# A statically scheduled kernel: the scheduler model holds the shared VectorE/GpSimd port longer, and its plan is searched anew with more weight on low TensorE activity

## Chip, cores, metric

One core of one Trainium2 chip. The metric is the device time of one execution in microseconds, as the median of several. Ratios are the mean time of one kernel's fast runs over that of the other's of the same rounds, so not quite the ratio of the medians quoted beside them.

## The reference

Four residual blocks on x of shape 1×2048×512: attention A, linear attention B, then both again.

```python
def _A_ref(x, wq, wk, wv, wo):            # 32 heads of 16, one shared K and V
    q = ...; k = x @ wk; v = x @ wv
    p = _softmax(einsum("bhqd,bkd->bhqk", q, k) * Dh ** -0.5)
    return (p @ v) @ wo                   # reshapes cut
def _B_ref(x, wqkv, wo):
    phi = lambda t: where(t > 0, t + 1, exp(t)) + 1e-6
    ...                                   # num = phi(q) @ (phi(k)^T v), den = phi(q) . sum phi(k)
    return (num / den) @ wo
x = x + A(layernorm(x)); x = x + B(layernorm(x))      # twice
```

The weight lies in A: 32 heads × 2048 × 2048 scores to exponentiate, twice. "Layer" below is one A with its B. The "boundary" is the stretch from the last exponential of layer 1 to the twenty-first of layer 2, the "tail" what follows the last exponential of layer 2.

## The kernel before

A Python list scheduler runs before launch. It plays the whole program on a clock of its own, with a duration for each op, and so decides the order on each engine and, for the attention tiles, which engine exponentiates what. The orders are then emitted with semaphores. The chip cannot change them. The scores of both layers are 4096 tiles of 512 columns. ScalarE takes sets of three or two (`exp`), VectorE takes single tiles (`P1`, an integer approximation), then adds three shifted copies of four such tiles, two by a wide op of its own (`xo`) and the last by four small GpSimd ops (`xp`); TensorE weighs all four.

```python
PLAN = (                      # every 6 us of the scheduler's clock: priorities, look-aheads, limits
    (0.0, {'LX': 0.338, 'HOLD': 0.836, 'LEAD': 16, ...}),
    (6.0, {'MF': 0.758, 'PX': 0.523, ...}),
    ...                       # cut: 245 entries
)
# Sched._try: may engine e start op o now? (cut)
if e == DV and o.port and self.tfree[PO] > self.now + 1e-9 or e == PO and self.dport > self.now + 1e-9:
    continue                  # VectorE's port ops and GpSimd exclude each other
...
# run(): engines are asked in this order at each event
self.engs = [PE, AC, DV, PO, SP]
...
# ScalarE's exponential, VectorE's P1, its shift, GpSimd's pieces (cut)
oe = add(AC, tac(m * 512), lambda e: e.activation(PTA[...], bank(...), ACTF.Exp, scale=SCALE), ...)
o = add(DV, tdv(512), lambda e: e.tensor_scalar(out=PTD[...512], in0=bank(db), ...), name="P1", ...)
o = add(DV, tdv(512 * m, 0.26), ..., name="xo", port=True)        # 2048 columns, SBUF to SBUF
add(PO, PXO[0] + 512 * PXO[1], ..., name="xp", pair=PXM)
...
# layer B, each of 16 token tiles: numerator's phi(q) times 1/den, on whichever engine is free
o = add((DV, PO) if PQE else DV, {DV: tdv(512), PO: PHS}, ..., name="pqn", port=True)
```

`tdv(512)` and the wide shift are 0.600 us in the model, `tac(1536)` 1.331 and `tac(1024)` 0.905, PHS 1.27.

The softmax here doesn't subtract the row's maximum and nothing guards it: scores larger than these inputs give would overflow.

## Time and profile before

| | before |
|---|---|
| median of 3 runs | 1495.28 us (1494.65 to 1497.23) |
| profiled run, first to last instruction | 1497.1 us |
| TensorE, ScalarE, VectorE, GpSimd busy | 97, 97, 92, 57% |

In profile lines PE is TensorE, PEld its weight loads, ACT ScalarE, DVE VectorE and POOL GpSimd; `out<-in` names the tiles, L1035 is line 1035 of the kernel. `ps_all` holds TensorE's results (in PSUM), which the program cuts into banks of 512 columns; `PTA` and `PTD` hold the exponentials (in SBUF). The prediction shows the page's busy line, its clock, its chain and the windows around the half clock. The table of waits (who waited for whom: total us, times, longest) says that TensorE's score loads wait mostly for a bank that an exponential still reads, then for P1:

```profile
PEld ps_all L1035 <- ACT PTA L1192: 220.1, 589, 0.9
...
PEld ps_all L1035 <- DVE PTD L1252: 88.5, 284, 0.7
```

And the view of line 1578, the multiplication `pqn` (count: shortest/median/longest ns, first and last start):

```profile
L1578 POOL TENSOR_TENSOR pqT<-pqT,e_buf x20: 1157/1162/1172, 733.1 to 1491.0; 128x512 bf16<-128x512 bf16 x20
L1578 DVE TENSOR_TENSOR pqT<-pqT,e_buf x12: 684/692/1048, 734.1 to 1492.3; 128x512 bf16<-128x512 bf16 x12
```

The two engines share the 32 multiplications; GpSimd needs 1.7 times as long for one. VectorE's longest, 1048 ns, began 0.5 us before a GpSimd op ended.

### The profile page before, as it was taken

Reading aid. Unit: us, or ns where it says so; the run is one execution under the profiler, and the core shown is the slowest. Engines: PE = TensorE matmul, PEld = TensorE weight load, DVE = VectorE, ACT = ScalarE, POOL = GpSimd, SP = SyncE. Lnnn points to the kernel's source line nnn. Section 1 sums busy time; section 2 is a strip of 40 time slices with the busy share of each in tenths; the row PEclk is TensorE's granted clock in tenths of the full one; section 3 lists DMA queues with packets and bytes.
Section 4 is the critical chain, followed back from the end, with each engine's and each line's share of the span. In section 5 each row is a group of like instructions: output and inputs, shape, how many; then the busy total and the mean of one; then the engine's idle time right before and its main releaser. Section 6 shows DMA issues by size and latency. Waiting matters only on the chain.

```text
span 1497.1 us, 38261 instructions
## 1 busy us (share of the span) xinstructions
PE 1459.2 (97%) x16245; PEld 492.0 (33%) x16255; DVE 1376.5 (92%) x2433; ACT 1444.9 (97%) x1426; POOL 853.2 (57%) x1360
## 2 busy tenths in 40 slices
PE   7999999999999999999899999999999999999998
PEld 4322333322333333333442333333333232333334
DVE  7999998999988999899798999989999899989987
ACT  7999999999999999999698999999999999999996
POOL 3556656565563655565544556566565456565654
PEclk9999999999999999999998999999999999999999
DMA  3000000000000000000000000000000000000001
GB/s 118 26 9 5 9 12 5 5 5 4 14 6 7 5 5 17 9 8 9 2 1 5 5 9 8 9 5 5 5 5 15 6 5 5 9 16 8 6 9 57
DMA packets 46251, 17.71 MB, mean 12 GB/s; under 512 B 39936, under 2 KB 45568, under 8 KB 46080
## 3 DMA queue, kind: packets, MB, share of 16 engines
q1 hardware_dynamic: 46080, 15.27, 4.3%
q8 instruction: 127, 2.08, 0.6%
q14 instruction: 44, 0.36, 0.1%
HBM read 5.28 MB, written 2.10 MB: 5 GB/s over the span
## 4 chain that ended last, share of the span: by engine, by line
PE 58%; ACT 23%; DVE 19%; issue 1%; POOL 0%; DMA 0%; SPq 0%; ACTq 0%
PE ps_all L1072 24%; PE ps_all L1035 23%; ACT PTA L1192 20%; DVE PTD L1252 10%; PE ps_all L768 7%; DVE PTD L1323 5%; PE ps_all L772 2%; PE ps_all L1093 2%; DVE Eo L1084 1%; DVE stats L840 1%; ACT e_buf L1576 1%; ACT e_buf L1439 1%; ACT e_buf L1577 1%; DVE e_buf L1446 0%; DVE x_sb L1431 0%
## 5 line engine op out<-in xcount | busy, mean ns | idle before, releaser
L1192 ACT ACTIVATE PTA<-ps_all 128x1536 bf16<-128x1536 f32 (+1 forms) x1178 | 1357.8, 1292 | 18.7 <-PE ps_all L1035 15.0
L1313 POOL TENSOR_SCALAR PTD<-PTD 128x512 uint16<-128x512 uint16 x1124 | 683.2, 618 | 489.2 <-DVE PTD L1323 317.6
L1252 DVE TENSOR_SCALAR PTD<-ps_all 128x512 uint16<-128x512 f32 x1142 | 751.1, 680 | 69.9 <-PE ps_all L1035 65.4
L1035 PE MATMUL ps_all<-QT,Kr 32*128 32x512 bf16 x4141 | 658.6, 385 | 9.9 <-ACT PTA L1192 3.6
L1072 PE MATMUL ps_all<-PTD,Vaug 128*32 128x512 bf16 x4568 | 616.2, 386 | 5.8 <-DVE Eo L1084 5.2
L1072 PE MATMUL ps_all<-PTA,Vaug 128*32 128x512 bf16 x2954 | 533.8, 387 | 0.2
L1323 DVE TENSOR_SCALAR PTD<-PTD 128x2048 uint16<-128x2048 uint16 x577 | 403.6, 711 | 2.2
L1035 PEld LDWEIGHTS ps_all<-QT,Kr 32*128 32x128 bf16 x4141 | 169.1, 91 | 493.0 <-ACT PTA L1192 220.1
L1072 PEld LDWEIGHTS ps_all<-PTD,Vaug 128*32 128x32 bf16 x4568 | 158.6, 94 | 218.1 <-issue 141.5
L1072 PEld LDWEIGHTS ps_all<-PTA,Vaug 128*32 128x32 bf16 x2954 | 131.8, 94 | 145.8 <-issue 114.2
L768 PE MATMUL ps_all<-wqkv_sb,xnT 128*32 128x512 bf16 x960 | 72.5, 382 | 0.1
L1448 POOL TENSOR_SCALAR e_buf<-e_buf 128x512 f32<-128x512 f32 x60 | 36.8, 613 | 43.1 <-ACT e_buf L1439 23.9
L1446 DVE TENSOR_SCALAR e_buf<-ps_all 128x512 f32<-128x512 f32 x60 | 40.9, 685 | 14.3 <-ACT e_buf L1439 14.2
L1439 ACT ACTIVATE e_buf<-ps_all 128x512 f32<-128x512 f32 x64 | 41.7, 655 | 9.7 <-PE ps_all L772 6.5
L1450 POOL TENSOR_TENSOR pqT<-e_buf 128x512 bf16<-128x512 f32 x30 | 38.0, 1268 | 11.8 <-DVE PTD L1323 8.0
L1450 POOL TENSOR_TENSOR pk_tok<-e_buf 128x512 bf16<-128x512 f32 x30 | 38.1, 1272 | 10.5 <-DVE PTD L1323 9.4
L1084 DVE COPY Eo<-ps_all 128x512 f32<-128x512 f32 x62 | 42.3, 682 | 1.5 <-PE ps_all L1072 1.3
L840 DVE BATCH_NORM_STATS2 stats<-x_sb 128x6 f32<-128x512 bf16 x64 | 42.9, 678 | 0.5 <-DMA x_sb<-in_A_x_dram 0.2
L1093 PE MATMUL ps_all<-identf,Eo 128*128 128x128 f32 x256 | 42.4, 289 | 0.0
L768 PE MATMUL ps_all<-wo_sb,OT 128*32 128x512 bf16 x480 | 37.7, 382 | 0.0
L1578 POOL TENSOR_TENSOR pqT<-pqT,e_buf 128x512 bf16<-128x512 bf16 x20 | 23.2, 1164 | 25.1 <-ACT e_buf L1577 6.5
L929 POOL TENSOR_SCALAR Vaug<-Vaug 128x32 bf16<-128x32 bf16 x48 | 14.9, 311 | 32.1 <-DVE Vaug L925 15.5
(102 smaller groups left out, 686.2 us busy)
## 6 DMA issues: line engine op xcount, KB each, us to landing
out_dram<-x_sb SPq DMA_DIRECT2D x16, 128.0 KB, 1.7
OT<-Osb SPq DMA_TRANSPOSE x120, 2.4
xnT<-xn_buf SPq DMA_TRANSPOSE x120, 2.3
wqkv_sb<-in_B_wqkv_dram SPq DMA_DIRECT2D x4, 384.0 KB, 3.1
x_sb<-in_A_x_dram SPq DMA_DIRECT2D x3, 256.0 KB, 3.4
x_sb<-in_A_x_dram SPq DMA_DIRECT2D x1, 768.0 KB, 7.9
wq_sb<-in_A_wq_dram SPq DMA_DIRECT2D x1, 512.0 KB, 6.4
x_sb<-in_A_x_dram SPq DMA_DIRECT2D x1, 512.0 KB, 8.7
```

Source lines behind the costliest of these rows:

```text
L768: i = e.matmul(out[32 * c:32 * c + 32], lhsT=lhsT[:, 32 * c:32 * c + 32], rhs=rhs, start=start, stop=stop, skip_group_check=True)
L840: add(DV, tdv(512), lambda e: e.bn_stats(stats[:, t, 0:6], x_sb[:, t, :]), reads=[("x", t)], writes=[("st", t)], prio=prio, name="bn")
L1035: x = e.matmul(bank(b0 + k), lhsT=Kr[r, m, kt * P:(kt + 1) * P], rhs=QT[r, self.units[u][0] % 2, gs, q0:q0 + n], start=True, stop=True)
L1072: return e.matmul(ps[32 * c:32 * c + 32, 7 * 512:8 * 512], lhsT=Vaug[:, kt, r, :], rhs=src() if callable(src) else src, start=opened[0], s ...
L1084: return (e.copy if oe.eng == AC else e.tensor_copy)(Eo[:, he.idx, :], bank(7))
L1093: i = e.transpose(bank(ht.idx, P, qs * P), Eo[:, he.idx, qs * P:(qs + 1) * P], identf[:])
L1192: oe = add(AC, tac(m * 512), lambda e: e.activation(PTA[:, hp.idx, 0:m * 512], bank(SETS[s][0], m * 512), ACTF.Exp, scale=SCALE), deps=[o] ...
L1252: o = add(DV, tdv(512), lambda e: e.tensor_scalar(out=PTD[:, hp.idx, i * 512:(i + 1) * 512], in0=bank(db), scalar1=SCALE * LOG2E * 128.0, ...
L1313: return e.tensor_scalar(out=PTD[:, ht.idx, i * 512:(i + 1) * 512], in0=PTD[:, hp.idx, i * 512:(i + 1) * 512], scalar1=float(SHIFT[r]), sc ...
L1323: return e.tensor_scalar(out=PTD[:, ht.idx, 0:512 * m], in0=PTD[:, hp.idx, 0:512 * m], scalar1=float(SHIFT[r]), op0=ALU.add, **kw)
L1439: o1 = add(AC, tac(512), lambda e: e.activation(e_buf[:, he.idx, :], bank(h.idx), ACTF.Exp), deps=[o], uses=[h], acq=[he] if fast else [he ...
L1450: add(PO, PHS, lambda e: e.tensor_tensor(out=dst, in0=sh(e_buf[:, hr.idx, :]), in1=sh(e_buf[:, he.idx, :]), op=ALU.add), deps=[o2, o3], us ...
```

## The change

Intent: make the model's port rule as slow as the chip's, and search the plan anew with an objective that punishes stretches in which TensorE does little (the prediction shows one of 13.65 us at half clock). The code (parameters cut; most of the 245 entries differ):

```diff
+PBL = 0.04
+R0 = 0
 PLAN = (
-    (0.0, {..., 'NT0': 3, 'DMIN': 1, ..., 'MF': 0.285, ..., 'PX': 2.788, ...}),
+    (0.0, {..., 'NT0': 5, 'DMIN': 2, ..., 'MF': 0.413, ..., 'PX': 0.523, ...}),
     ... (cut)
-            if e == DV and o.port and self.tfree[PO] > self.now + 1e-9 or ...
+            if e == DV and o.port and self.tfree[PO] > 0.0 and self.tfree[PO] + PBL > self.now + 1e-9 or ...
+        if e == PO:
+            self.at(end + PBL, None)
-   ... self.add_pv(p, ..., dep[0 if r and not split else i], r, 1)
+   ... self.add_pv(p, ..., c["p1"][-1] if R0 and not r else dep[0 if r and not split else i], r, 1)
```

The new wait of 0.04 us (PBL) before a VectorE port op is called the hold below. R0 is 0, so the last edit does nothing. Two lines were added near the top and two in the body: old line 1252 is new 1256, 1323 is 1327, 1578 is 1582.

## The prediction

> **What bounds the kernel now.** I read the page's busy shares first, then the slices, the groups by line, the table of waits, and short windows of the timeline.
>
> ```profile
> PE 1459.2 (97%) x16245; PEld 492.0 (33%) x16255; DVE 1376.5 (92%) x2433; ACT 1444.9 (97%) x1426; POOL 853.2 (57%) x1360
> ...
> PEclk9999999999999999999998999999999999999999
> ...
> PE 58%; ACT 23%; DVE 19%; issue 1%; POOL 0%; DMA 0%; SPq 0%; ACTq 0%
> ```
>
> Three engines are nearly full, and the chain of waits passes between them. There is no single bound. A Python list scheduler lays out, before launch, one fixed order for each engine. ScalarE (ACT) takes the exponentials of score tiles in sets of three or two; VectorE (DVE) takes the others through an integer approximation: one op from PSUM ("P1", line 1252), two shifts over four tiles (line 1323), while GpSimd (POOL) does the fourth shift in pieces (line 1313). What matters is how far the chip departs from the times the scheduler assumed, since the orders cannot adapt. For that I compare starts of neighbours, which are not hidden by the overlap of ends. An exponential of three tiles follows its neighbour after 1331 ns at the median, one of two after 904 ns, and a P1 takes 600 ns from end to end: just the assumed durations. One group is off:
>
> ```profile
> L1252 DVE TENSOR_SCALAR PTD<-ps_all 128x512 uint16<-128x512 f32 x1142 | 751.1, 680 | 69.9 <-PE ps_all L1035 65.4
> L1323 DVE TENSOR_SCALAR PTD<-PTD 128x2048 uint16<-128x2048 uint16 x574 | 402.6, 713 | 2.2
> ```
>
> Both are assumed at 600 ns, yet the shift's mean is 713 ns and P1's 680. Sorting the 574 shifts by whether a GpSimd op still ran at their start gives two piles: 286 that start 150 to 200 ns before a GpSimd op ends have a mean of 728 ns; the 195 whose start meets no GpSimd op have 679. From end to end a shift takes 600 or 647 ns, mean 632. One pair in the timeline (VectorE, then GpSimd):
>
> ```profile
> 805.61 0.72 DVE L1323 TENSOR_SCALAR PTD<-PTD 128x2048 uint16<-128x2048 uint16 x1
> 806.26 1.27 DVE L1252 TENSOR_SCALAR PTD<-ps_all 128x512 uint16<-128x512 f32 x2
> ```
> ```profile
> 803.98 1.81 POOL L1313 TENSOR_SCALAR PTD<-PTD 128x512 uint16<-128x512 uint16 x3 [0.63 <-DVE PTD L1323]
> ```
>
> GpSimd ends at 803.98+1.81 = 805.79, 0.18 us after the shift's start; the shift ends at 806.33, and the next op starts 0.65 us after it instead of 0.60. Last, the dip in PEclk:
>
> ```profile
> 780.00:810.00 30.00, 30.00 (x313) 9.20 (x310) 26.93 (x46) 28.62 (x26) 15.73 (x26) 1.00 0.01 1
> 810.00:830.00 20.00, 19.52 (x147) 4.54 (x144) 14.83 (x25) 14.21 (x13) 8.34 (x15) 0.66 0.05 9
> 830.00:860.00 30.00, 29.64 (x311) 9.27 (x310) 29.51 (x53) 29.79 (x27) 17.89 (x30) 1.00 0.03 5
> ```
>
> The clock record has one stretch of 13.65 us at half speed, from 813.0. ScalarE (fourth busy number) is idle for 20-14.21 = 5.8 us there; around it it is idle for 60-58.41 = 1.6 us in 60, or 0.5 in 20. So the stretch cost about 5.3 us.
>
> **What the Trainium skill says.** "SBUF — State Buffer", section "Who interferes with whom": VectorE's second pair of SBUF ports is GpSimd's pair; it is an exclusive lock held for a whole instruction, and the later of the two blocks. `tensor_scalar` in a two-port mode takes it, an op with at most one SBUF input outside those modes does not. The trace agrees: shifts behind a GpSimd op lose 49 ns, P1 (PSUM input) shows 683 ns with GpSimd running and 678 without. "VectorE: DVE Perf Modes", section "Mode 4×_2P — both tricks at once", explains why the shift is such an op: 16-bit SBUF to SBUF, one source; it moves 2048 elements in the 600 ns that P1 takes for 512. "TensorE: Matmul & The Clock Gate", section "What's actually happening": a free-running window of activity of about 3.4 us halves the clock when TensorE was little used and restores it after a busy one. The trace agrees that the clock has only 1.0 and 0.5, and that one thin spell was enough.
>
> **The change part by part.** The emitted instructions are the same in kind; only the scheduler's clock and 200-odd lines of tuned parameters differ. The new R0 is 0 and does nothing. So I compare the two built programs' counts and orders.
>
> (a) The port. The model now forbids a VectorE port op until 0.04 us after GpSimd's end: close to the 47 ns measured. The hardware wait is not abolished: 574 × (632-600) = 18.4 us on VectorE stay, unless another op (a P1) runs in the gap. What improves is that the plan expects it, so TensorE's in-order queue is no longer stuck behind a late P1 while ScalarE's next scores wait. I bound the prize: in 20-700 and 840-1450 us the starts after ScalarE's exponentials are later than 1331/904 ns by 18.8 + 15.6 = 34.4 us in sum. Some of this is planned (evictions, projections). I choose a quarter as recovered: -9 us.
>
> (b) Shares. The exponentials go from 598 of three and 580 of two to 601, 582 and one of a single tile: 14 of 4096 tiles move from VectorE to ScalarE (P1 1142 to 1128). ScalarE gains 3×1.331 + 2×0.904 + 0.48 = +6.3 us; its other ops nearly cancel. VectorE sheds 14×0.60 = 8.4 us of P1, some six shifts, and (d). As ScalarE is as full as TensorE, I count two thirds as showing in the end: +4 us.
>
> (c) Clock. If no stretch of half speed remains, -5.3 us. A search that punishes thin spells makes this likely, not certain, as the window is free-running and the new order's spells are unknown; at 0.55, -3 us. The small filler matmuls rise from 44 to 100 (11 to 25 groups), full ones fall from 28 to 17: the new plan still has thin places and pads more.
>
> (d) A side effect: when GpSimd becomes free, it may start at once but VectorE not for 0.04 us, so GpSimd takes all 32 multiplications of line 1578 (before 20, VectorE 12). They cost 1162 against 692 ns; in the last layer 16 of them at 1.12 us apart are 17.9 us, about as long as that phase (first normaliser 1474.5, last VectorE one 1492.3). I count +1 us.
>
> (e) TensorE: four small matmuls share one pass of about 0.217 us. The approximate tiles shed 56 matmuls (-3.0 us), the exponentials add 14 (+0.8), fillers 56 small (+3.0) and 11 full (-2.4), scores 23 (+1.7 at three a pass): 0.
>
> Sum: 1495.3 - 9 + 4 - 3 + 1 = 1488.3 us.
>
> **Rivals.** *The wait is only moved.* VectorE still loses 47 ns behind GpSimd and now the model also leaves gaps, so VectorE takes fewer tiles and ScalarE more. For it: 14 tiles moved, and VectorE is idle for 8% anyway, so a 47 ns loss may have been absorbed already. Against it: waits of the score loads on P1 already sum to 88.5 us in 284 cases. The time would be 1495 + 4 to 6 = 1499 to 1501. *All of it lands.* If half of the 34.4 us is recovered, the low clock goes and the shift of shares is free, it is 1495 - 17 - 5 = 1473. Against it: much of the 34.4 us comes from work that the counts show unchanged. *The clock decides.* A new plan could trip the gate somewhere else, or twice; each costs some 5 us. Then -9 + 4 + 1 + 5 gives about 1496.
>
> **Range and chances.** The rivals span 1473 to 1501. Repeats of the kernel before stay within 2.6 us, so noise adds little; the spread is my choice of fractions. I take 1479 to 1498, and lean to faster since each edit removes an error of the model that the trace shows. A change of 2% is 30 us: more than the port's 18.4 and the clock's 5.3 us together. Faster by over 2%: 0.015. Slower by over 2%: would need 30 us lost with the same instructions: 0.01. Within: 0.975.
>
> **What would show it.** Right: ScalarE's excess over 1331/904 ns falls from 34 to about 25 us; no stretch of half clock; ScalarE's busy time up by 4 to 7 us and VectorE's down by 15 or more, while the span falls. For step (a): still many shifts at 647 ns end to end, but fewer late P1, and less waiting of score loads on line 1252's successor than 88.5 us. Wrong: if the shifts' mean falls to 600 ns, the wait was hidden rather than planned; if the excess stays at 34 us while the time falls, the gain came from clock or layer boundaries (700-840 us); if a second stretch at half clock appears, step (c) has the wrong sign.

## The result

| | before | after |
|---|---|---|
| first measurement, median | 1496.26 us (4 runs) | 1498.34 us (4 runs, 3 of them fast) |
| five rounds (e1), median | 1495.22 us (1494.28 to 1496.39) | 1498.25 us (1497.81 to 1498.83) |

The ratio of e1 is 1.0020 with a 95% interval of 1.0008 to 1.0033: the changed kernel is 0.2% slower. That is "same" at 2%, but 0.3 us outside the stated range of 1479 to 1498 and on the other side of the kernel before. The first profiled run of the changed kernel was slow (1570.17 us, granted clock 0.829). It is set aside; the views below are of e1's trace, at clock 1.000.

Page of the changed kernel (e1): busy times, then the chain that ended last.

```profile
PE 1458.8 (97%) x16267; PEld 495.2 (33%) x16281; DVE 1353.3 (90%) x2397; ACT 1451.6 (97%) x1435; POOL 864.3 (58%) x1368
...
ACT 47%; PE 44%; DVE 7%; POOL 1%; issue 1%; DMA 0%; POOLq 0%; SPq 0%; ACTq 0%
```

ScalarE has 6.7 us more to do, VectorE 23 us less, and the chain has moved from TensorE (58 to 44%) to ScalarE (23 to 47%). P1 and the shift by shape, and the waits:

```profile
L1256 DVE TENSOR_SCALAR PTD<-ps_all 128x512 uint16<-128x512 f32 x1128 | 744.4, 681 | 76.9 <-PE ps_all L1039 71.1
...
L1327 DVE TENSOR_SCALAR PTD<-PTD 128x2048 uint16<-128x2048 uint16 x562 | 389.0, 706 | 2.6
```
```profile
PEld ps_all L1039 <- ACT PTA L1196: 231.1, 614, 0.9
...
PEld ps_all L1039 <- DVE PTD L1256: 66.7, 222, 0.7
```

The shift's mean fell only from 713 to 706 ns: 248 shifts still start 150 to 200 ns before a GpSimd op ends and have a mean of 730 ns; end to end the mean is 627 ns (632 before). TensorE waits 22 us less for P1 and 11 us more for exponentials. The stretch at half clock is gone (windows: PE, PEld, DVE, ACT, POOL busy, then clock):

```profile
810.00:830.00 20.00, 19.77 (x205) 6.66 (x205) 19.56 (x33) 19.97 (x19) 11.95 (x20) 1.00 0.04 9
```

ScalarE is busy 19.97 of 20 us there, against 14.21. So much of what was predicted did appear. The lag of the chip is its time less the planned time of the same op; the slip of a phase is what the lag grows by in it. Where did the gain go? The scheduler knows when it meant each op to start, so I laid its clock beside the trace: the n-th exponential of the plan is the n-th of the trace. The plan of the kernel before ends at 1473.9 us, that of the changed kernel at 1481.1. The chip lags both. In steps (e15 is a trace of the kernel before without a half clock in layer 2):

| step | plan before | plan after | chip before (e15) | chip after (e1) |
|---|---|---|---|---|
| start to 10th exponential | 31.5 | 32.0 | 33.2 | 34.6 |
| to the last exponential of layer 1 | 668.7 | 670.6 | 678.6 | 681.2 |
| boundary: to the 21st of layer 2 | 73.9 | 77.0 | 73.8 | 77.0 |
| to the last exponential of layer 2 | 656.7 | 656.5 | 665.4 | 663.4 |
| tail: to the end | 43.2 | 45.0 | 41.8 | 40.8 |
| sum | 1473.9 | 1481.1 | 1492.8 | 1497.0 |

The first row varies from trace to trace (33.0 to 33.8 us with the old order, 33.3 to 34.6 with the new), and e15's tail holds 3.4 us of half clock; without it the tail before took 40.8 us. What is left: the two attention phases together +0.6 us, the boundary +3.2 us. The plan itself became longer, and in the boundary the chip follows it. (The expectations call the boundary's end the twentieth exponential and give 77.1 and 40.9 for 77.0 and 40.8.)

### The profile page after: what moved, and what is told of

Same layout as the page of the kernel before. It is cut to its first block, busy times and chain, and to the rows that moved or that the text cites. A ratio compares the mean times of both kernels' runs of the same rounds, so it can differ in the third digit from the quotient of the medians.

```text
span 1568.5 us, 38304 instructions
## 1 busy us (share of the span) xinstructions
PE 1542.3 (98%) x16281; PEld 491.1 (31%) x16281; DVE 1364.5 (87%) x2397; ACT 1474.8 (94%) x1435; POOL 864.2 (55%) x1368
## 4 chain that ended last, share of the span: by engine, by line
PE 83%; DVE 9%; ACT 8%; issue 0%; DMA 0%; SPq 0%
PE ps_all L1076 35%; PE ps_all L1039 30%; PE ps_all L772 10%; ACT PTA L1196 7%; DVE PTD L1256 4%; PE ps_all L776 4%; PE ps_all L1097 2%; DVE PTD L1327 2%; DVE Eo L1088 1%; PE ps_all L875 0%; DVE stats L844 0%; DVE Msb L1559 0%; DVE e_buf L1450 0%; DMA x_sb<-in_A_x_dram 0%; PE ps_all L1380 0%
## 5 line engine op out<-in xcount | busy, mean ns | idle before, releaser
L1196 ACT ACTIVATE PTA<-ps_all 128x1536 bf16<-128x1536 f32 (+1 forms) x1184 | 1380.1, 1250 | 53.3 <-PE ps_all L1039 46.6
L1076 PE MATMUL ps_all<-PTD,Vaug 128*32 128x512 bf16 x4512 | 667.7, 417 | 3.3 <-DVE Eo L1088 2.3
L1076 PE MATMUL ps_all<-PTA,Vaug 128*32 128x512 bf16 x2968 | 577.2, 413 | 0.0
L1327 DVE TENSOR_SCALAR PTD<-PTD 128x2048 uint16<-128x2048 uint16 (+1 forms) x568 | 388.9, 699 | 2.6
L1039 PEld LDWEIGHTS ps_all<-QT,Kr 32*128 32x128 bf16 x4164 | 154.5, 91 | 527.4 <-issue 241.6
L772 PE MATMUL ps_all<-wqkv_sb,xnT 128*32 128x512 bf16 x960 | 82.8, 418 | 0.1
L1452 POOL TENSOR_SCALAR e_buf<-e_buf 128x512 f32<-128x512 f32 x58 | 35.5, 613 | 37.0 <-ACT e_buf L1443 18.4
L1582 POOL TENSOR_TENSOR pqT<-pqT,e_buf 128x512 bf16<-128x512 bf16 x32 | 36.8, 1164 | 25.2 <-ACT e_buf L1581 16.0
L844 DVE BATCH_NORM_STATS2 stats<-x_sb 128x6 f32<-128x512 bf16 x64 | 43.2, 680 | 0.9 <-DMA x_sb<-in_A_x_dram 0.6
L772 PE MATMUL ps_all<-wo_sb,OT 128*32 128x512 bf16 x480 | 41.8, 417 | 0.0
L776 PE MATMUL ps_all<-Msb,pqT 128*128 128x512 bf16 x128 | 36.4, 421 | 1.1 <-DVE Msb L1559 1.1
```

What stands on the lines that cost most here:

```text
L772: i = e.matmul(out[32 * c:32 * c + 32], lhsT=lhsT[:, 32 * c:32 * c + 32], rhs=rhs, start=start, stop=stop, skip_group_check=True)
L776: return e.matmul(out, lhsT=lhsT, rhs=rhs, start=start, stop=stop, skip_group_check=True)
L844: add(DV, tdv(512), lambda e: e.bn_stats(stats[:, t, 0:6], x_sb[:, t, :]), reads=[("x", t)], writes=[("st", t)], prio=prio, name="bn")
L1039: x = e.matmul(bank(b0 + k), lhsT=Kr[r, m, kt * P:(kt + 1) * P], rhs=QT[r, self.units[u][0] % 2, gs, q0:q0 + n], start=True, stop=True)
L1076: return e.matmul(ps[32 * c:32 * c + 32, 7 * 512:8 * 512], lhsT=Vaug[:, kt, r, :], rhs=src() if callable(src) else src, start=opened[0], s ...
L1196: oe = add(AC, tac(m * 512), lambda e: e.activation(PTA[:, hp.idx, 0:m * 512], bank(SETS[s][0], m * 512), ACTF.Exp, scale=SCALE), deps=[o] ...
```

## Experiments

Runs e1 to e4, e9 to e11, e15 and e16 keep every order of one of the two kernels; e5 and e6 do so up to the tail, e7, e13 and e14 up to the boundary between the layers. "Plan" means the scheduler's own clock. e7, e8 and e12 to e16 were timed once, so their state stays unknown; what is read from the traces of e7 and e13 to e16 lies in stretches at full clock unless it says otherwise.

**e1: the changed kernel again.**

> The changed kernel unaltered, to get a trace in the fast state and a tight ratio. Two programs' scheduler plans end at 1473.9 us (before) and 1481.1 us (after) by the scheduler's own clock, so I look at the lag of the chip behind the plan. Theory P (plan longer, lag shorter): ratio 1.000 to 1.003, no stretch at half clock, lag at the end about 15 us against about 22 before, and its steady slope a little smaller. Rival S (port wait moved, not planned away): the slope of the lag is as before (about 1.3 us per 100 us) and the whole lag gain is the missing 6 us step of the half clock. Rival C (clock): a stretch at half clock somewhere eats the gain; the mean clock would be below 0.997.

Measured: 1498.25 us, ratio 1.0020, no half clock. The plan's end is lagged by 16 us, before by 23 with the half clock of the first trace and 19 in e15. In the two attention phases of the table the exponentials slip 17.5 us behind their plan, before 18.6 us. So theory P holds in kind: the plan is 7 us longer, the lag shorter; but the slip shrank by 1.1 us only, so rival S, that it stays, is nearly as close.

**e2 and e3: GpSimd's pieces cut short, so that no shift meets one.** The same edit in both kernels; the result is wrong, beyond tolerance in e2 only. The memset keeps the unwritten columns defined.

```diff
-    add(DV, 0.3, lambda e: e.memset(one5[:], 1.0), ...)
+    add(DV, 0.3, lambda e: (e.memset(PTD tails [416:512], 0), e.memset(one5[:], 1.0))[-1], ...)
-    e.tensor_scalar(out=PTD[:, ht.idx, i * 512:(i + 1) * 512], in0=PTD[:, hp.idx, i * 512:(i + 1) * 512], ...)
+    e.tensor_scalar(out=PTD[:, ht.idx, i * 512:i * 512 + 416], in0=PTD[:, hp.idx, i * 512:i * 512 + 416], ...)
```

> Kernel before with the same orders, but GpSimd's shift pieces cover 416 of 512 columns, so that each ends about 0.1 us earlier than planned and no VectorE shift meets it (wrong result on purpose; a memset of the tails at the start costs up to 5 us once). Theory P/port: shifts end to end fall from 632 to 600 ns and the steady lag of the chip behind the plan (about 17 us without the clock step) falls by more than half, 9 us or more. Rival A (absorbed): shifts fall to 600 ns but the lag slope stays, since VectorE's 8% idle time took the waits; the time changes only by the memset's 2 to 5 us.

> The same shortening in the changed kernel. Theory P/port: its plan already holds 0.04 us for the port, so the lag falls less than in the kernel before, by 0 to 4 us. Rival A: as little as before in both.

Shift by shape in e2, then in e3:

```profile
L1323 DVE TENSOR_SCALAR PTD<-PTD 128x2048 uint16<-128x2048 uint16 x574 | 387.3, 687 | 2.2
```
```profile
L1327 DVE TENSOR_SCALAR PTD<-PTD 128x2048 uint16<-128x2048 uint16 x562 | 377.1, 685 | 2.6
```

Both means are now at the level of unblocked shifts; end to end 602 ns. The port wait is all but gone (in e2 11 shifts of 574 still start more than 200 ns before a GpSimd op ends), 17 us of VectorE time before and 14 after. The time barely moved: 1495.24 us (ratio 1.0001, memset of 2.4 us at the start included) and 1497.98 us. The slip behind the plan in the attention phases fell from 18.6 to 15.6 us and from 17.5 to 15.4. So the port wait cost the kernel before at most 3.0 us (at most, since a shorter piece also ends sooner for TensorE), and the changed kernel 2.1. The hold bought about 0.9 us. Rival A was nearly right: VectorE's idle time absorbs most of the wait. Theory P's "9 us or more" falls.

**e4: the kernel before, with score matmuls doubled ahead of the half clock.**

```diff
+            t_now = sc.now
             def f(e):
+                if 795.0 < t_now < 804.0:
+                    self.smm(e, got, SETS[s][0])
```

> Kernel before with the same orders; score matmuls of ScalarE's sets are issued twice for the nine sets planned between 795 and 804 us (about 806 to 815 on the chip), to lift TensorE's activity just ahead of the stretch at half clock. If the thin spell trips the gate and the stretch costs the 6 us that the lag shows, the stretch disappears and the time falls by 4 to 6 us (ratio 0.996 to 0.9975); the result stays correct. Rival: the doubled matmuls delay TensorE as much (9 x 0.22 to 0.65 us), or the gate trips elsewhere: ratio 0.999 to 1.003.

Measured: correct, 1497.42 us, ratio 1.0012 (0.9997 to 1.0027). There is no stretch near 812 us in its trace, but the doubling itself cost something: between 775 and 825 us the lag grows by 2.2 us (12.8 to 15.0), in e15 without a stretch by 1.1, and layer 2 took 666.9 us against 665.4. It is no improvement, and since the stretch is not there in every run (below), this single trace does not show that the filling removed it.

**e15 and e16: the kernel before.** No edit.

> The kernel before once more, for its clock record. Theory C (the fall to half clock near 812 us comes and goes from run to run and costs 5 us when it comes): either a stretch near 812 us and a second layer of about 671 us (twentieth exponential excluded: last exponential of layer 2 less the twentieth), or none and about 665 us.

> As the run before it: about 671 us with the stretch at half clock, about 665 us without.

Windows of e15, then e16:

```profile
810.00:830.00 20.00, 19.52 (x202) 5.86 (x200) 19.23 (x34) 18.97 (x17) 10.50 (x18) 1.00 0.04 9
```
```profile
810.00:830.00 20.00, 19.52 (x167) 5.15 (x165) 17.07 (x30) 16.39 (x15) 9.88 (x17) 0.83 0.05 9
```

One without a stretch (second layer 665.4 us), one with 6.83 us of it (668.3). With 13.65 us in the first trace it was 670.7, so a stretch costs 2.9 and 5.3 us. Of seven traces with this order near 812 us (the first, e2, e5, e9, e10, e15, e16) three had it: 13.65, 30.72 and 6.83 us. Of four fast traces with the changed order (e1, e3, e6, e11) none has one between the boundary and the last exponential. Averaged over the first, e5, e15 and e16, whose orders and work there are the same, it costs (5.3 + 0 + 0 + 2.9)/4, about 2 us a run. A thin spell alone does not bring it: in the 3.41 us before 813.0 us e15 started as many matmuls (24) as the first trace, and its clock stayed.

Seven and four traces are few, but the record lists the granted clock of every timed run; 0.001 is about 3 us at half clock. In the rounds of the experiments the kernel before has 25 such runs, all fast:

| clock | runs | mean time |
|---|---|---|
| 0.999 | 14 | 1494.8 us |
| 0.998 | 6 | 1496.2 us |
| 0.997 | 3 | 1497.3 us |
| 0.995 | 2 | 1498.8 us |

A line through them gives 0.35 us per us at half clock, 1.9 us a run on average. All 21 fast runs of the changed order (first measurement, e1, e3, e6, e11) have 0.999 or 1.000. So the new order does avoid the longer stretches; short ones of 3.41 us remain in the boundary (e6, e11), as with the old order (e2, e4, e9, e10). At like clock the changed kernel is thus further behind than by 3.0 us.

**e5 and e6: GpSimd's share of `pqn` in the tail alone.** In e5 the kernel before gets all 16 of the last layer on GpSimd. In e6 the changed kernel drops the hold after its last exponential.

```diff
-  o = add((DV, PO) if PQE else DV, ...            # e5
+  o = add((DV, PO) if nxt is not None else PO, ...
+  sc.at(1436.5, lambda: globals().update({'PBL': 0.0}))   # e6
```

> Kernel before with one side effect of the change alone, in the last layer's tail: all 16 multiplications of line 1578 on GpSimd (before: 9 there, 7 on VectorE). The orders are the same up to there. The scheduler's own clock says +3.3 us (1477.3 against 1473.9). Theory G (the hold gives GpSimd these multiplications, and that costs): +2 to +3.5 us, ratio 1.0015 to 1.0025. Rival (the chip's tail hides it, since the last matmuls and transfers set its end; the tails of the two kernels measured alike, 40.9 and 40.7 us): within 1 us, ratio 1.000.

> The changed kernel with the hold of 0.04 us switched off from 1436.5 us of the plan on, after the last exponential: VectorE gets 5 of the 16 multiplications back. Plan 1477.6 against 1481.1. Theory G: 2 to 3.5 us faster than the changed kernel (about 1495.5, ratio to before 1.000). Rival: as the changed kernel, 1498 (ratio 1.002).

Measured: e5 1496.75 us, ratio 1.0007 (0.9993 to 1.0021); e6 1497.83 us, ratio 1.0011 (0.9998 to 1.0024), where the unedited changed kernel had 1.0020. In e5's trace the tail takes 43.7 us, 1.9 more than e15's 41.8 (both with 3.41 us at half clock); in e6's it takes 39.5, 1.3 less than e1's 40.8. Its view of line 1582:

```profile
L1582 POOL TENSOR_TENSOR pqT<-pqT,e_buf x27: 1157/1165/1171, 738.0 to 1490.9; 128x512 bf16<-128x512 bf16 x27
L1582 DVE TENSOR_TENSOR pqT<-pqT,e_buf x5: 685/685/866, 1476.9 to 1490.2; 128x512 bf16<-128x512 bf16 x5
```

Five multiplications went back to VectorE. About 1 to 2 us each way, a third to a half of what the plan says (3.3 and 3.5); neither interval of the times excludes zero by itself. The plan gives each multiplication on GpSimd 1.27 us; in e1's tail they follow each other after 1.12 us, which makes 16 of them 2.4 us shorter on the chip.

**e7: all 32 multiplications of the kernel before on GpSimd.**

```diff
-  o = add((DV, PO) if PQE else DV, ...
+  o = add(PO, ...
```

> Kernel before with all 32 of these multiplications on GpSimd, in both layers. Only the boundary between the layers is to be read from it (the second layer is thrown off, since its tuned parameters meet another state: plan 1505.9). From the last exponential of layer 1 to the twentieth of layer 2 the chip took 73.8 us before and 77.1 in the changed kernel. Theory G: about 76 us here (plan 76.2 against 73.9). Rival (the four tiles and other parameters of the boundary did it): about 74 us.

Measured: the boundary took 75.7 us (712.0 to 787.7), 1.9 more than before; theory G holds there. The whole took 1527.62 us, since the second layer's parameters met another state (plan 1505.9).

**e13 and e14: the changed kernel without the hold in the boundary.** e13 keeps its parameters there; e14 takes the old ones for that stretch, shifted by the 2.4 us that layer 1 ends later.

```diff
+  sc.at(703.0, lambda: globals().update({'PBL': 0.0}))
+  sc.at(790.0, lambda: globals().update({'PBL': 0.04}))
   # e14 also: old PLAN entries between 703 and 790
```

> The changed kernel with the hold off between 703 and 790 us of the plan only, its new parameters kept. Only the boundary is read (last exponential of layer 1 to the twentieth of layer 2: 73.8 us before, 77.1 changed; what follows is thrown off, plan 1506.0). If the hold alone made it long: about 74.5. If the new parameters are what sets it: about 77 (the plan says 76.9).

> The same, with the old table's parameters of that stretch too. Plan 74.8 us for the boundary. If hold and parameters together made it long: about 75 on the chip; if the state left by the new first layer is to blame: about 77.

The boundary took 76.7 us in e13 and 74.8 in e14 (77.0 with the change, 73.8 before). Without the hold but with parameters fitted to it, GpSimd still does 13 of the 16 multiplications and 0.3 us comes back; with both undone, the two engines share them exactly as before (11 and 5) and 2.2 of the 3.2 us come back. The last 1.0 us is there before the first multiplication: it starts 22.4 us after the last exponential in e14 and 21.4 before. So it comes from the state that the new layer 1 leaves; that part is not taken apart further. The whole runs, 1522.75 and 1533.42 us, say nothing (thrown-off second layer).

GpSimd in the boundary, in the kernel before and then in e1 (start, length, op, count, idle before):

```profile
733.13 1.16 POOL L1578 TENSOR_TENSOR pqT<-pqT,e_buf 128x512 bf16<-128x512 bf16 x1 [6.41 <-DVE Msb L1555]
735.69 4.94 POOL L1578 TENSOR_TENSOR pqT<-pqT,e_buf 128x512 bf16<-128x512 bf16 x4 [1.40 <-DVE pqT L1578]
740.82 1.16 POOL L1578 TENSOR_TENSOR pqT<-pqT,e_buf 128x512 bf16<-128x512 bf16 x1 [0.19 <-DVE stats L840]
```
```profile
737.77 3.40 POOL L1582 TENSOR_TENSOR pqT<-pqT,e_buf 128x512 bf16<-128x512 bf16 x3 [6.69 <-ACT e_buf L1581]
741.59 1.16 POOL L1582 TENSOR_TENSOR pqT<-pqT,e_buf 128x512 bf16<-128x512 bf16 x1 [0.41 <-DVE x_sb L1597]
742.90 3.41 POOL L1582 TENSOR_TENSOR pqT<-pqT,e_buf 128x512 bf16<-128x512 bf16 x3
746.58 1.16 POOL L1582 TENSOR_TENSOR pqT<-pqT,e_buf 128x512 bf16<-128x512 bf16 x1 [0.27 <-DVE mv L845]
```

Before, six multiplications run here and VectorE does others (the wait "DVE pqT" is one); after, GpSimd does eight in a row by itself. Each tile's chain to the next layer's first scores goes through this op.

**e8 and e12: each half of the change alone.** e8: new parameters, old rule. e12: old parameters, new rule.

```diff
 # e8: before + the new PLAN        # e12: after with the old PLAN
```

> Half of the change alone: the new table of parameters with the old port rule. The scheduler's own clock says 1532.8 us; with the chip's usual lag of 14 to 22 us that makes 1547 to 1555 us. If so, the two halves cannot be judged apart: a table fits only the rule that it was searched under. Rival: the chip doesn't care (table and rule are small), 1495 to 1505.

> The other half of the change alone: the hold of 0.04 us with the old table of parameters. The scheduler's own clock says 1560.1 us; with the lag of 17 to 22 us seen so far that makes 1577 to 1582 us. Rival (the rule alone is harmless on the chip, since the chip waits anyway): 1495 to 1510.

Measured: 1551.36 us (plan 1532.8) and 1582.05 us (plan 1560.1), both correct. The halves cannot be judged apart: each table fits only the rule that it was searched under. How much of the 7 us that the plan grew by is the hold's, and how much comes of a new search with another objective, is therefore not shown. The lag was 17 and 20 us from first to last instruction, so the plan foretold both.

**e9, e10, e11: what an engine's time is worth.** Exponentials 16 columns shorter (e9 before, e11 after), or P1 16 columns shorter (e10 before). Their outputs are wrong, which doesn't matter for the times. Same orders; a small memset as in e2.

```diff
-  e.activation(PTA[:, hp.idx, 0:m * 512], bank(SETS[s][0], m * 512), ...)              # e9, e11
+  e.activation(PTA[:, hp.idx, 0:m * 512 - 16], bank(SETS[s][0], m * 512 - 16), ...)
-  e.tensor_scalar(out=PTD[..., i * 512:(i + 1) * 512], in0=bank(db), ...)              # e10
+  e.tensor_scalar(out=PTD[..., i * 512:i * 512 + 496], in0=bank(db, 496), ...)
```

> Kernel before with the same orders; every exponential of ScalarE covers 16 columns less (13.3 ns each by the 0.8325 ns a column of the scheduler, 1178 of them: 15.7 us less work on ScalarE; wrong result on purpose; a small memset at the start, under 1 us). Theory B (ScalarE is the bound in the attention phases, so its 6.3 us more in the changed kernel should show): 8 to 15 us faster, ratio 0.990 to 0.995. Rival W (the engines wait for each other in turn; one alone is worth little): 0 to 5 us faster, and the moved tiles cost as little.

> Kernel before with the same orders; every P1 of VectorE covers 496 of 512 columns (16.6 ns each at 1.04 ns a column, 1142 of them: 19 us less work on VectorE; wrong result on purpose). Theory B (VectorE has slack): 0 to 3 us faster. Rival V (VectorE's lateness feeds the chain, so port waits should matter too): 5 us or more faster, ratio below 0.997.

> The same cut of ScalarE's exponentials (1184, 15.7 us) in the changed kernel, which planned 13.0 us of idle time behind ScalarE's exponentials against 16.8 before. Theory B: it gains more than the kernel before does, by 1 to 4 us. Rival W: both gain alike, 0 to 5 us.

Measured: 1490.84 us (ratio 0.9982, interval 0.9944 to 1.0021), 1492.40 (0.9981), 1490.67 (0.9965). By the medians e9 gained 4.2 us (in rival W's range), e10 2.6 (theory B's: VectorE has slack) and e11 7.6 against e1 (3.4 more than e9, theory B's). e9's interval is wide because one of its runs, 1501.89 us, lies far off; its trace has 30.72 us at half clock. The undisturbed phases say more. e9's layer 1 fell from 678.6 to 676.3 us for about 7.9 us less ScalarE work: 0.3 us per us. e11's two attention phases fell from 681.2 + 663.4 to 677.6 + 659.8: 7.2 us for 15.7, or 0.46. e10's fell from 678.6 + 665.4 to 677.0 + 664.0: 3.0 us for 19, or 0.16. Neither theory B nor W holds in full: ScalarE's time counts for a third to a half, VectorE's for a sixth. In the changed kernel ScalarE counts for more, which agrees with the chain (ACT 47%) and with the plan's idle time behind exponentials (13.0 us, 16.8 before).

## Why the prediction was wrong

- **What bounds the kernel.** Right: no single bound. e9 to e11 put numbers on it.
- **(a) The port, "-9 us": the failing step.** The lock, its 47 ns and the 18.4 us of VectorE time were right, and so was the remark that the wait stays. What failed was taking the 34.4 us of late starts behind exponentials as the pool and "a quarter as recovered". The plan holds 16.8 us of that itself; 17.6 are slip. Removing the port wait almost altogether moves 3.0 us (e2). The change gained 1.1 us in slip, about 0.9 of it by the port. The excess did fall, to 30.9 us (17.7 + 13.2), but by about as much as the plan's own idle time fell (16.8 to 13.0), and that time ScalarE now fills with more tiles. A VectorE op that ends 47 ns late costs the end about a sixth of that; e10's 0.16 would have turned 18.4 us into 3.
- **(b) Shares, "+4 us".** Counts right: ScalarE +6.7 us busy (4 to 7 stated), VectorE -23 (15 or more). The weight was too high, and the relief of VectorE was not credited. With e9 to e11's weights, 6.3 × 0.3 to 0.46 is 2 to 3 us, less about 3 us for some 17 us of VectorE work, so about 0; the attention phases came out at +1.7 us in the plan and, with the smaller slip, +0.6 on the chip.
- **(c) Clock, "-3 us".** Sign right: no fast run of the changed order has a clock below 0.999, and the price of the stretch seen was 5.3 us. But the kernel before pays it in some runs only, about 2 us on average, and I treated one trace as typical. That -3 came near -2 is partly luck: the reckoning was one long stretch avoided at odds of 0.55, while the record has shorter ones in some runs, all avoided.
- **(d) GpSimd takes all multiplications, "+1 us".** The mechanism was foreseen and is on the trace (32 of 32). I counted it in the tail, where it costs 1 to 2 us (e5, e6) and yet the two tails came out alike (40.8 us), and forgot the boundary, where the next layer waits for the same op: 1.9 us when forced on the kernel before, 2.2 us back when hold and parameters are undone there.
- **(e) TensorE, "0".** Its busy time is 1458.8 against 1459.2 us. Half clock lengthens it (1456.0 in e15), and e3, with the matmuls of e1, has 1454.7; so 0 within 4 us.

The sum by measured terms: attention +0.6, boundary +3.2, clock -2.0, tail 0, start +1.4 in these two traces, which is about what it varies by anyway. That is +1.8 to +3.2 us; timed, +3.0. Of the rivals, "the wait is only moved" gave 1499 to 1501 us and came nearest, with the wrong reason for most of it: not VectorE's gaps in the attention phases but the layer boundary.

No run with a correct result and orders other than those of the kernel before is faster than it, so there is no better version to offer. That a new search with the hold applied to the shifts alone, not to `pqn`, would keep the clock's 2 us and drop the boundary's 2 is argued, not tried: e8 and e12 show that it needs a full search.

## What to carry to other kernels

Correcting a scheduler's model makes its plan honest before it makes it shorter: check what the corrected cost is worth at the end (shorten the op on the chip with the orders fixed) before making every decision pay for it. A rule that delays one engine at an instant when another is free also decides who takes shared work, so count such ops per engine after each change. Lay the plan's clock beside the trace; steps at equal milestones show in a minute whether the plan or the lag moved.

## What the Trainium skill lacked or had wrong

- "SBUF — State Buffer", "Who interferes with whom": the lock is there as stated, but the page gives no cost for an op that comes just behind the holder. Here a 2048-column shift took 647 ns end to end instead of 600, in about half of the cases; and in this kernel 18.4 us of such waits were worth at most 3.0 us.
- "TensorE: Matmul & The Clock Gate", "What's actually happening": the half-clock stretches in these traces are 3.41, 6.83, 10.24, 13.65 and 30.72 us, whole multiples of the page's window of 3.413 us, so it agrees. What it lacks is an example of chance in mid-kernel: the same instruction order fell to half clock near 812 us in three of seven traces, for 6.83 to 30.72 us.
- The same page, "Seeing it yourself", has a limiter at 13/16 (0.8125) that one or two busy cores never trip. One run of this one-core program, at 1570 us, recorded 0.752 for 356 us from its start on and then 0.850 for 1202 us; neither is 0.8125, and the run was 4.8% longer than the others. What else ran on that die is not known.
